# Second layer's first product of a two-layer feed-forward kernel as seven half-size products

## The chip, the cores and the metric

The program runs on one core of a Trainium2 chip. The metric is the device time of one execution in microseconds (us). The core's TensorE (PE) does the matrix products, VectorE (DVE) and ScalarE (ACT) the elementwise work, GpSimd (POOL) a little of the attention, and SyncE (SP) issues all transfers. Products go into PSUM, eight banks of 512 float32 columns on 128 partitions; everything else lies in SBUF.

## The reference

```python
def reference(...):
    x = attention(q, k, v, lam)                  # decayed linear attention
    x = x.transpose(...).reshape(1536, 512)      # tokens x features
    h = x @ moe_w_in                             # layer 1: 512 -> 2048
    x = (h * tanh(softplus(h))) @ moe_w_out      #          2048 -> 512
    h = x @ moe2_w_in                            # layer 2: 512 -> 2048
    g = h * clip(h + 3.0, 0.0, 6.0) / 6.0
    return g @ moe2_w_out                        #          2048 -> 512
```

## The kernel before

The 1536 tokens are three blocks of 512 (k = 0, 1, 2) and the 2048 hidden features sixteen tiles of 128. An operand is kept as two float32r parts, a high one (`split_hi`, ACT) and the rest (`split_lo`, DVE), and a product is three passes over the parts: high-high, high-low, low-high (`PASS`). So one 128x128 weight tile against 512 tokens takes three matmuls.

**Layer 1** is 48 steps of the loop `for n in range(STEPS)`: `gemm1` (12 matmuls of 512 columns, line 328), two steps later `emit_g2` (12 more, line 337), with Mish on ACT between them (lines 357, 358) and `g_lo` on DVE. Blocks 0 and 1 go through tiles 0 to 7 first and leave their sums in `part` ("keep"), block 2 goes through all sixteen and is split at once into X[2] ("split"), then blocks 0 and 1 go through tiles 8 to 15 ("add", line 372), and `split_owed` splits their sums into X[0] and X[1].

From step 21 on `make_later` also prepares layer 2's weights between the steps. Such a unit is one half (0: first product, 1: second product) of one pair p of tiles. `assemble` rebuilds it from its loaded 64-bit form (lines 296 to 302); of the second product's half it makes four sums (line 462). `deliver` splits it into a slot of `low` and spills it to HBM (`wc`). Half 0 has four 128x512 parts of weights, half 1 has seven.

**Layer 2** is 24 runs j, one for each block and pair: block 2, 0, 1, eight pairs each, in turning order so that pairs still in SBUF are used again. Four slots of both halves are held, the others are fetched from `wc` (`swap`). A run's first product (line 609) is two times 12 matmuls of 512 columns into one PSUM bank. `gate` applies relu, min and multiply (lines 632, 633), `sums` makes four sums of the 2x2 blocks of tokens by features (line 643), `parts` splits seven 128x256 blocks (lines 86, 89). The second product (line 625) is already Strassen's scheme (in Winograd's form): seven products m = 1 to 7, each of two times three matmuls of 256 columns, 42 in all, kept in seven PSUM banks through the eight pairs of a block. It follows one run behind the first product: of run j - 1, products 1, 4, 2 stand behind the first half of run j's first product, products 6, 7, 5, 3 behind the second half. At a block's end `close` scales and adds the seven banks into four quarters of the output and stores them.

A scheduler may move instructions on each engine, so the order of the code is only nearly that of the queues.

Of the kernel before, what the change touches and what calls it, by code (L numbers as in the profile page):

```python
# [20 lines left out]
def decay_attention__mish_ffn__hswish_ffn_kernel(  # L21
# [8 lines left out]
    nc = tc.nc  # L30
# [37 lines left out]
    BANKS = {"h": 2, "y": 4, "a": 2}  # L68

    def bank(kind, shape, name):  # L70
        i = bank_turn[kind]
        bank_turn[kind] = (i + 1) % BANKS[kind]
        return ps.tile(shape, F32, tag=f"{kind}{i}", name=name)
# [92 lines left out]
    def scores(c, kind):  # L166
        qT, kT = qk(c)
        sc = [bank(kind, [128, 4, 128], f"sc{h2}") for h2 in range(2)]
# [96 lines left out]
    def load_w(w, t, half, count):  # L265
        if w is w1 and count == 2:
            st = stage_p.tile([128, 2, 512], U64, tag="st2", name="st")
        elif w is w1:
            i = unit_turn[0] % 3
            unit_turn[0] += 1  # L270
            slots[w is w1, t, half] = {i}
            st = ring[:, i:i + 1]
        elif half == 0:
            slots[w is w1, t, half] = {0, 1}
            st = ring[:, 0:2]
        else:
            slots[w is w1, t, half] = {3}
            st = spare[0][:, 8:16].bitcast(U64).rearrange("p a n -> p (a n)").rearrange("p (t n) -> p t n", t=2)
# [33 lines left out]
    def convert(w, t, half, count):  # L312
        hf = to_single(staged(w, t, half))
        cols = slice(half * 512, half * 512 + 512)
        if count == 2:
            whole, i = (low0, t) if t < 2 else (low, t - 2)
            both = whole.rearrange("p (t a n) -> p t a n", a=2, n=1024)[:, i:i + 2, :, cols]
            wh, wl = both[:, :, 0], both[:, :, 1]
        else:
            wh, wl = W[t][:, 0:1, cols], W[t][:, 1:2, cols]  # L320
        split(wh, wl, hf)
# [42 lines left out]

    def evacuate(n, es):
        layer, k, t, first, last, end = seq[n]
        for e in es:
# [5 lines left out]
            else:  # L373
                split_hi(X[k][:, 0, e, :], y)
                split_lo(X[k][:, 1, e, :], X[k][:, 0, e, :], y)
            if end == "add":
                owed.append((k, e))

    owed = []

    def split_owed():
        if owed:
            k, e = owed.pop(0)
            split_hi(X[k][:, 0, e, :], part[k][:, e, :])
            split_lo(X[k][:, 1, e, :], X[k][:, 0, e, :], part[k][:, e, :])

    def emit_g2(n):
        layer, k, t, first, last, end = seq[n]
        if first:
            y_t[:] = [bank("y", [128, 512], "y") for _ in range(4)]  # L390
        gemm2(layer, t, g_t.pop(n), y_t, first, last, range(4))
        if last:
            evacuate(n, range(4))
# [58 lines left out]
    def assemble(u):  # L452
        p, half = later[u]
        B = spare[0] if half else ring[:, 2].bitcast(F32).rearrange("p (a n) -> p a n", n=256)
        whole = B[:, 0:4].rearrange("p (t i) n -> p t (i n)", t=2)
        to_single(staged(w2, 2 * p, half), whole)
        prefetch(u + 3)
        if half == 0:
            ready[u] = whole
        else:  # L460
            for o, x, y in ((4, 0, 1), (5, 2, 4), (6, 2, 0), (7, 3, 5)):
                nc.vector.tensor_tensor(out=B[:, o], in0=B[:, x], in1=B[:, y], op=ALU.subtract)
            ready[u] = B[:, 1:8]

    def deliver(u):
        p, half = later[u]
        c = w2c(p % 2) if half else w1c(p % 2).rearrange("p t a n -> p a t n")
        split(c[:, 0], c[:, 1], ready.pop(u))
        spill(p, half)
# [53 lines left out]
    twice = {24, 27, 31, 35, 39, 43}  # L523
    chunk = {"s": 4, "o": 4}
    for n in range(STEPS):
# [23 lines left out]
        h = bank("h", [128, 512], "h")  # L549
# [21 lines left out]
        split_owed()  # L571
        if n not in conv_first:
            advance(conv_at.get(n, 0))
        if n == 20:
            spare.append(main.tile([128, 16, 256], F32, tag="low0", name="spare"))
            prefetch(2)
        if n >= 21 and PHASES:
            make_later(2 if n in twice else 1)

    SLOT += [(up[0][:, 2048 * i:2048 * i + 2048], up[1 + 2 * i][:, 0:3584]) for i in range(2)]  # L580
    assert not PHASES
    GBUF = [main.tile([128, 4096], F32R, tag="low0", name="G0")[:, 0:3584], up[2][:, 0:3584]]
# [227 lines left out]
```

## Time and profile before

| | us |
|---|---|
| median of 3 timed runs | 584.03 (582.09 to 584.14) |
| profiled execution | 580.44 |
| its span, first to last instruction | 578.7 |
| of this: attention and layer 1 | 0 to 313.6 |
| layer 2, 24 runs | 313.6 to 573.2 |
| last sums and stores | to 578.7 |

The profile is of one execution. Its time is 1.74 us more than its span, and the timed runs lie up to 3.7 us above it. A matmul's end in the records is modelled, so matmuls that follow one another overlap by some 0.16 us in the busy times; the start of one to the start of the next is the safer measure.

### The profile page before, as it was taken

Reading aid. Unit: us, or ns where it says so; the run is one execution under the profiler, and the core shown is the slowest. Engines: PE = TensorE matmul, PEld = TensorE weight load, DVE = VectorE, ACT = ScalarE, POOL = GpSimd, SP = SyncE. Lnnn points to the kernel's source line nnn. Section 1 sums busy time; section 2 is a strip of 40 time slices with the busy share of each in tenths; the row PEclk is TensorE's granted clock in tenths of the full one; section 3 lists DMA queues with packets and bytes.
Section 4 is the critical chain, followed back from the end, with each engine's and each line's share of the span. In section 5 each row is a group of like instructions: output and inputs, shape, how many; then the busy total and the mean of one; then the engine's idle time right before and its main releaser. Section 6 shows DMA issues by size and latency. Waiting matters only on the chain.

```text
span 578.7 us, 8451 instructions
## 1 busy us (share of the span) xinstructions
PE 567.0 (98%) x3470; PEld 479.9 (83%) x3470; DVE 350.2 (61%) x516; ACT 258.5 (45%) x371; POOL 15.6 (3%) x20
## 2 busy tenths in 40 slices
PE   7999999999999999999999999999999999999996
PEld 3777787778888888888888888899989988999895
DVE  3799963465747677675881645355654554754555
ACT  2379733345756557565751333233232333332332
POOL 1600100000000000000000000000000000000000
PEclk9999999999999999999999999999999999999999
DMA  7968622422445879667896568400487300585302
GB/s 236 410 235 294 243 75 74 182 74 91 141 170 218 321 297 323 272 219 297 323 362 256 199 232 312 183 1 1 146 306 294 128 0 19 185 323 221 128 1 73
DMA packets 23168, 113.80 MB, mean 197 GB/s; under 512 B 2122, under 2 KB 6234, under 8 KB 17498
## 3 DMA queue, kind: packets, MB, share of 16 engines
q1 hardware_dynamic: 23130, 113.26, 53.0%
q8 instruction: 27, 0.44, 0.3%
q14 instruction: 11, 0.09, 0.1%
HBM read 87.03 MB, written 26.22 MB: 196 GB/s over the span
## 4 chain that ended last, share of the span: by engine, by line
PE 86%; DVE 5%; ACT 3%; DMA 2%; POOL 1%; issue 1%; DVEq 0%; SPq 0%; POOLq 0%; ACTq 0%
PE h L609 22%; PE h L328 21%; PE y L337 20%; PE acc L625 20%; ACT st L296 1%; PE uo L217 1%; DMA mask<-z 1%; PE sc L172 1%; PE uo L226 1%; PE uo L210 1%; DVE low L89 1%; POOL raw L188 1%; POOL raw L190 0%; DVE X L89 0%; DVE raw L195 0%
## 5 line engine op out<-in xcount | busy, mean ns | idle before, releaser
L633 DVE SCALAR_TENSOR_TENSOR F<-x,h 128x512 f32<-128x512 f32 x48 | 33.0, 687 | 95.1 <-ACT x L632 95.0
L632 ACT ACTIVATE x<-h 128x512 f32<-128x512 f32 x48 | 28.7, 598 | 124.9 <-PE h L609 124.7
L328 PE MATMUL h<-X,low 128*128 128x512 f32 x288 | 71.9, 397 | 0.2 <-DVE state L249 0.2
L609 PE MATMUL h<-X,up 128*128 128x512 f32 x288 | 70.0, 392 | 0.3 <-DVE F L633 0.3
L337 PE MATMUL y<-g,low 128*128 128x512 f32 x288 | 69.8, 390 | 0.1
L609 PE MATMUL h<-X,low 128*128 128x512 f32 x288 | 69.8, 391 | 0.0
L328 PE MATMUL h<-X,up 128*128 128x512 f32 x288 | 69.2, 389 | 0.0
L337 PE MATMUL y<-g,up 128*128 128x512 f32 x288 | 69.2, 389 | 0.0
L337 PEld LDWEIGHTS y<-g,low 128*128 128x128 f32 x288 | 53.9, 188 | 12.1 <-DVE low L89 1.0
L328 PEld LDWEIGHTS h<-X,low 128*128 128x128 f32 x288 | 52.9, 188 | 13.2 <-issue 1.9
L328 PEld LDWEIGHTS h<-X,up 128*128 128x128 f32 x288 | 54.1, 188 | 11.2
L337 PEld LDWEIGHTS y<-g,up 128*128 128x128 f32 x288 | 54.1, 188 | 11.2
L609 PEld LDWEIGHTS h<-X,up 128*128 128x128 f32 x288 | 52.5, 188 | 10.4 <-DVE F L633 0.5
L609 PEld LDWEIGHTS h<-X,low 128*128 128x128 f32 x288 | 52.7, 188 | 10.0
L357 ACT ACTIVATE x<-h 128x512 f32<-128x512 f32 x48 | 28.5, 594 | 65.8 <-PE h L328 65.8
L89 DVE TENSOR_TENSOR g<-x,g 128x512 fp32r<-128x512 f32 x48 | 33.0, 687 | 41.0 <-ACT g L358 40.9
L296 ACT ACTIVATE ring<-ring 128x512 f32<-128x512 f32 (+3 forms) x52 | 40.0, 826 | 14.3 <-DMA ring<-w 14.3
L643 DVE TENSOR_TENSOR F<-F 128x256 f32<-128x256 f32 x96 | 40.6, 423 | 2.2
L86 ACT ACTIVATE up<-F 128x768 fp32r<-128x768 f32 (+3 forms) x27 | 23.5, 871 | 25.4 <-DVE F L643 15.6
L86 ACT ACTIVATE G<-F 128x768 fp32r<-128x768 f32 (+1 forms) x24 | 22.9, 954 | 25.7 <-DVE F L643 16.6
L89 DVE TENSOR_TENSOR up<-F,up 128x768 fp32r<-128x768 f32 (+3 forms) x27 | 26.6, 988 | 12.4 <-ACT up L86 12.4
L625 PEld LDWEIGHTS acc<-low,G 128*128 128x128 f32 x252 | 31.9, 191 | 1.8 <-ACT G L86 0.6
(65 smaller groups left out, 692.1 us busy)
## 6 DMA issues: line engine op xcount, KB each, us to landing
wc<-low SPq DMA_DIRECT2D x8, 1792.0 KB, 6.7
up<-wc SPq DMA_DIRECT2D x8, 1792.0 KB, 7.4
raw<-att SPq DMA_DIRECT2D x24, 512.0 KB, 6.4
low<-wc SPq DMA_DIRECT2D x6, 1792.0 KB, 7.3
ring<-w SPq DMA_DIRECT2D x18, 512.0 KB, 5.0
ring<-w SPq DMA_DIRECT2D x8, 1024.0 KB, 5.0
spare<-w SPq DMA_DIRECT2D x8, 1024.0 KB, 6.1
wc<-low SPq DMA_DIRECT2D x8, 1024.0 KB, 8.8
```

What stands on the lines that cost most here:

```text
L86: nc.scalar.activation(out=hi, in_=src, func=ACTF.Copy)
L89: nc.vector.tensor_tensor(out=lo, in0=src, in1=f32(hi), op=ALU.subtract)
L172: nc.tensor.matmul(sc[h2][:, p, :], lhsT=kT[r, p, :], rhs=qT[r, p, :], start=True, stop=True)
L296: ins = nc.scalar.activation(out=o, in_=i, func=ACTF.Copy, scale=scale, bias=bias)
L328: nc.tensor.matmul(h, lhsT=W[t][:, a, kt * 128:kt * 128 + 128], rhs=X[k][:, b, kt, :], start=(kt, a, b) == order[0], stop=(kt, a, b) == or ...
L337: nc.tensor.matmul(y[e], lhsT=l, rhs=r, start=(first and i == 0), stop=(last and i == 2),)
L357: nc.scalar.activation(out=x, in_=h, func=ACTF.Mish)
L609: nc.tensor.matmul(h, lhsT=w[:, a, kt * 128:kt * 128 + 128], rhs=X[k][:, b, kt, :], start=(kt, a, b) == order[0], stop=(kt, a, b) == order ...
L625: nc.tensor.matmul(acc[m][:, s], lhsT=G[:, a, gi, s * 128:s * 128 + 128], rhs=w[:, b, wi], start=(first and s == 0 and i == 0), stop=(last ...
L632: nc.scalar.activation(out=x, in_=h, func=ACTF.Relu, bias=3.0)
L633: nc.vector.scalar_tensor_tensor(out=F[:, 2 * i:2 * i + 2].rearrange("p i n -> p (i n)"), in0=x, scalar=6.0, in1=h, op0=ALU.min, op1=ALU.mult,
L643: nc.vector.tensor_tensor(out=F[:, o], in0=F[:, a], in1=F[:, b], op=op)
```

## The change

The first product of layer 2 becomes seven products as well: tokens (512 into 2x256), input features (512 into 2x256) and hidden features (2 tiles) are halved. Each is 128 features by 256 tokens over 256 inputs: two tiles times three passes, six matmuls of 256 columns, 42 a run in place of 24 of 512. The operands are seven sums of the weights (`WSUMS`, now for half 0 too, so both halves are alike: seven parts, 1792 KB) and seven of the tokens (`token_sums`, in `XC`). They go in four fills, a (product 1), b (2, 6), c (7, 5) and d (4, 3), through bank 0 one after the other. Each is copied out by ACT, DVE adds the copies up into the two tiles' 2x2 blocks `FH`, and the gate then works in SBUF. Behind each fill stand products of the second product, which now lags by two runs (`LAG`). The units of weights are reordered (the half-0 units of the last two pairs come last), six slots of one unit are held, and four fetches are issued within layer 1 (`EARLY`).

```diff
-    BANKS = {"h": 2, "y": 4, "a": 2}
+    BANKS = {"h": (0, 1), "y": (2, 3, 4, 5), "a": (6, 7)}
...
+    GROUP_BANKS = [(2, 3, 4, 5)] * 3 + [(6, 7, 2, 3), (4, 5, 6, 7)]
...
+        if end == "split":
+            y = BANK[:, b:b + 4]
+            nc.scalar.activation(out=tmp[:, 0], in_=y[:, 0:2, 256:512], func=ACTF.Copy)
+            for _ in token_sums(k, y, tmp):
+                pass
...
+    def token_sums(k, y, tmp=None):     # seven put, four sub, one at a time
+        def sub(o, a, b):
+            nc.vector.tensor_tensor(out=o, in0=a, in1=b, op=ALU.subtract)
+        def put(i, src):
+            split(xs[i][:, 0], xs[i][:, 1], src)
...
+    later = [(p, half) for p in range(NPAIR - 2) for half in (0, 1)]
+    later += [(p, half) for half in (1, 0) for p in (NPAIR - 2, NPAIR - 1)]
...
     def assemble(u):
-        if half == 0:
-            ready[u] = whole
-        else:
-            for o, x, y in ((4, 0, 1), (5, 2, 4), (6, 2, 0), (7, 3, 5)):
+        for o, x, y, op in WSUMS[half]:
+            nc.vector.tensor_tensor(out=B[:, o], in0=B[:, x], in1=B[:, y], op=op)
+        ready[u] = B[:, 1:8]
     def deliver(u):
-        split(c[:, 0], c[:, 1], ready.pop(u))
-        spill(p, half)
+        split(c[:, :, 0], c[:, :, 1], ready.pop(u))
+        spill(later[u], u % 2)
...
+    EARLY = {43: ((3, (NPAIR - 3, 0)),), 45: ((4, (NPAIR - 1, 1)),), 47: ((5, (NPAIR - 2, 1)), (2, (NPAIR - 4, 0)))}
...
-        split_owed()
...
+    LAG = 2
+    FILLS = (("a", (1,)), ("b", (2, 6)), ("c", (7, 5)), ("d", (4, 3)))
+    ACC = {1: 2, 4: 3, 2: 1, 6: 4, 7: 5, 5: 6, 3: 7}
+    def fill(j, ms, bank_):
+        for i, m in enumerate(ms):
+            for kt in range(2):
+                for q, (a, b) in enumerate(PASS):
+                    nc.tensor.matmul(
+                        bank_[:, 256 * i:256 * i + 256], lhsT=w[:, a, kt * 128:kt * 128 + 128], rhs=x[:, b, kt],
...
+    GAPS = ((1,), (4, 2), (6, 7), (5, 3))
+    for j in range(R):
+        if j == 0:
+            prepare.append(token_sums(0, part[0]))
+        if j == NPAIR + 1:
+            prepare.append(token_sums(1, part[1]))
+        for f, (name, ms) in enumerate(FILLS):
+            bank_ = BANK[:, f % 2 if j < LAG else 0]
+            fill(j, ms, bank_)
+            nc.scalar.activation(out=c, in_=bank_[:, 0:n], func=ACTF.Copy)
+            if f == 1:    # one add of 512 columns; f == 2: of 512 and 256; f == 3: of 512
...
+            if j < LAG:
+                emit_g2(STEPS - 2 + j, [f])
+            else:
+                second(j - LAG, GAPS[f])
+            if f == 0 and j > 0:
+                gate(j - 1, 0, 3)
+                feature_sums(j - 1)
+            elif f == 1 and j > 0:
+                feature_parts(j - 1)
+            elif f == 3:
+                gate(j, 1, 1)
+            if f in (1, 3):
+                for g in prepare:
+                    next(g, None)
+        for x in swaps.get(j, ()):
+            fetch(*x)
```

TensorE's queue in run 3 of layer 2 before: two halves of the first product (L609, 12 matmuls each), each followed by products of the second (L625).

```order
L609 MATMUL h_2782<-X2_78,up0_81 128x512 [waits DMAHW4_49,DVE_49]
L609 MATMUL h_2782<-X2_78,up0_81 128x512 x11
L625 MATMUL acc1_2618<-up1_818,G0_2520 128x256 [waits DMAHW0_49,Activation_49]
L625 MATMUL acc1_2618<-up1_818,G0_2520 128x256
L625 MATMUL acc1_2618<-up1_818,G0_2520 128x256 [waits DVE_49]
L625 MATMUL acc1_2618<-up1_818,G0_2520 128x256 x3
L625 MATMUL acc4_2625<-up1_818,G0_2520 128x256 x6
L625 MATMUL acc2_2632<-up1_818,G0_2520 128x256 x6
L609 MATMUL h_2817<-X2_78,up0_81 128x512 [waits DVE_49]
L609 MATMUL h_2817<-X2_78,up0_81 128x512 x11
```

TensorE's queue after the change in run 8 (the first run of block 0), from fill a (L698 is `fill`, L712 `second`).

```order
L698 MATMUL bank_76<-X0_77,lowA_81 128x256 [waits Activation_49]
L698 MATMUL bank_76<-X0_77,lowA_81 128x256 x5
L712 MATMUL bank_76<-up0_82,lowB_2453 128x256 [waits DMAHW6_49]
L712 MATMUL bank_76<-up0_82,lowB_2453 128x256
L712 MATMUL bank_76<-up0_82,lowB_2453 128x256 [waits DVE_49]
L712 MATMUL bank_76<-up0_82,lowB_2453 128x256 x3
L698 MATMUL bank_76<-X0_77,lowA_81 128x256 [waits Activation_49]
L698 MATMUL bank_76<-X0_77,lowA_81 128x256 x5
L698 MATMUL bank_76<-X1_78,lowA_81 128x256 x6
L712 MATMUL bank_76<-up0_82,lowB_2453 128x256 x12
L698 MATMUL bank_76<-X1_78,lowA_81 128x256 [waits Activation_49]
```

Between two fills stand six or twelve matmuls of the second product, and each fill's first matmul waits for ACT, which copies the fill before it out of the same bank.

The same queue in run 7, from fill a.

```order
L698 MATMUL bank_76<-X2_79,lowA_81 128x256 [waits DMAHW4_49,Activation_49]
L698 MATMUL bank_76<-X2_79,lowA_81 128x256 x5
L698 MATMUL bank_76<-X2_79,lowA_81 128x256 [waits Activation_49]
L698 MATMUL bank_76<-X2_79,lowA_81 128x256 x5
L698 MATMUL bank_76<-lowA_81 128x256 x6
L712 MATMUL bank_76<-lowA_81,up3_1228 128x256 [waits DMAHW5_49]
L712 MATMUL bank_76<-lowA_81,up3_1228 128x256
L712 MATMUL bank_76<-lowA_81,up3_1228 128x256 [waits DVE_49]
L712 MATMUL bank_76<-lowA_81,up3_1228 128x256 x15
```

Here the scheduler has put fill b directly behind fill a, and the six matmuls of product 1 behind fill b; so it is, in whole or in part, in runs 4, 5 and 7.

ScalarE's queue after the change through run 6 (L813 copies fills out, L722 is the gate's relu, L88 `split_hi`).

```order
L813 ACTIVATE work_2457<-bank_76 128x256 [waits PE_49,Activation_49]
L88 ACTIVATE lowB_2453<-work_2457 128x3x256 [waits DVE_49]
L813 ACTIVATE work_2457<-bank_76 128x512 [waits PE_49,Activation_49]
L88 ACTIVATE lowB_2453<-FS1_2540 128x4x256 [waits DVE_49]
L813 ACTIVATE two_2458<-bank_76 128x512 [waits PE_49,Activation_49]
L722 ACTIVATE x_3056<-work_2457 128x512 [waits DVE_49,Activation_49]
L813 ACTIVATE two_2458<-bank_76 128x512 [waits PE_49,Activation_49]
L722 ACTIVATE x_3074<-work_2457 128x512 [waits DVE_49]
L813 ACTIVATE work_2457<-bank_76 128x256 [waits PE_49,Activation_49]
```

The four copies a, b, c, d of a run stand in one queue with two splits and two relus, each of which waits for DVE; before, this queue held two relus and two splits a run and no copy.

## Rows read from the trace of the kernel before

**Rows 1.** The page: busy us of each engine (share of the span, instructions)
```profile
PE 567.0 (98%) x3470; PEld 479.9 (83%) x3470; DVE 350.2 (61%) x516; ACT 258.5 (45%) x371; POOL 15.6 (3%) x20
```
**Rows 2.** Stages by windows: length, busy us of each engine, clock, DMA share, GB/s
```profile
224.00:313.60 89.60, 89.60 (x397) 74.20 (x396) 62.26 (x78) 51.66 (x68) 0.00 (x0) 1.00 0.81 303
313.60:347.00 33.40, 32.69 (x182) 28.27 (x181) 17.42 (x30) 10.31 (x15) 0.00 (x0) 1.00 0.51 188
347.00:557.50 210.50, 210.50 (x1323) 190.92 (x1322) 111.06 (x175) 65.44 (x86) 0.00 (x0) 1.00 0.42 155
```
**Rows 3.** The chain that ended last, one run of layer 2 and its end: start, us
```profile
354.80 2.87 PE acc L625 x24
357.67 2.75 PE h L609 x12
360.42 2.15 PE acc L625 x18
...
565.30 5.05 PE acc L625 x42
```
**Rows 4.** Timeline of TensorE where layer 2 begins: start, us, what
```profile
313.61 2.88 PE L609 MATMUL h<-X,low 128*128 128x512 f32 x12
...
324.49 2.88 PE L609 MATMUL h<-X,low 128*128 128x512 f32 x12
...
336.34 0.96 PE L609 MATMUL h<-X,up 128*128 128x512 f32 x3 [0.28 <-DVE F L633]
```
**Rows 5.** The chain where TensorE waits in run 1: start, us, what
```profile
329.86 0.04 issue
329.90 1.22 PE acc L625 x8
```
**Rows 6.** Timeline near the end, a first product's half and its gate
```profile
560.24 2.32 PE L625 MATMUL acc<-up,G 128*128 128x256 f32 x18
560.50 0.60 ACT L632 ACTIVATE x<-h 128x512 f32<-128x512 f32 x1 [1.00 <-PE h L609]
561.13 0.69 DVE L633 SCALAR_TENSOR_TENSOR F<-x,h 128x512 f32<-128x512 f32 x1 [0.37 <-ACT x L632]
```
**Rows 7.** Groups by shape, whole span: count, busy us and mean ns, idle before
```profile
L632 ACT ACTIVATE x<-h 128x512 f32<-128x512 f32 x48 | 28.7, 598 | 124.9 <-PE h L609 124.7
L643 DVE TENSOR_TENSOR F<-F 128x256 f32<-128x256 f32 x96 | 40.6, 423 | 2.2
L89 DVE TENSOR_TENSOR G<-F,G 128x1024 fp32r<-128x1024 f32 x12 | 14.7, 1225 | 10.1 <-ACT G L86 10.1
L86 ACT ACTIVATE G<-F 128x1024 fp32r<-128x1024 f32 x12 | 12.7, 1060 | 16.6 <-DVE F L643 16.6
L89 DVE TENSOR_TENSOR G<-F,G 128x768 fp32r<-128x768 f32 x12 | 11.5, 960 | 0.0
L86 ACT ACTIVATE G<-F 128x768 fp32r<-128x768 f32 x12 | 10.2, 848 | 9.1 <-DVE F L633 9.1
L86 ACT ACTIVATE X<-uo 128x256 fp32r<-128x256 f32 x24 | 8.6, 380 | 23.8 <-PE uo L226 16.4 <-DVE state L251 5.7 <-PE uo L217 1.0
L89 DVE TENSOR_TENSOR X<-part,X 128x512 fp32r<-128x512 f32 x8 | 5.4, 684 | 0.0
```
**Rows 8.** Groups of the preparation of layer 2's weights, whole span
```profile
L462 DVE TENSOR_TENSOR spare<-spare 128x256 f32<-128x256 f32 x32 | 12.1, 419 | 0.2
L89 DVE TENSOR_TENSOR low<-spare,low 128x1792 fp32r<-128x1792 f32 x8 | 16.2, 2024 | 8.6 <-ACT low L86 8.6
L89 DVE TENSOR_TENSOR low<-ring,low 128x1024 fp32r<-128x1024 f32 x8 | 9.7, 1219 | 0.5 <-ACT low L86 0.5
```
**Rows 9.** Timeline of DVE: the last unit of weights delivered
```profile
300.91 2.03 DVE L89 TENSOR_TENSOR low<-spare,low 128x1792 fp32r<-128x1792 f32 x1 [1.77 <-ACT low L86]
```
**Rows 10.** DMA issues: queue, count, KB each, median us from issue to landing
```profile
wc<-low SPq DMA_DIRECT2D x8, 1792.0 KB, 6.7
up<-wc SPq DMA_DIRECT2D x8, 1792.0 KB, 7.4
```

More of the change, by code (lines that the diff above doesn't have):

```diff
@@ L167, in scores @@
         qT, kT = qk(c)
-        sc = [bank(kind, [128, 4, 128], f"sc{h2}") for h2 in range(2)]
+        sc = [bank(kind, [128, 4, 128]) for h2 in range(2)]
         for p in range(4):
@@ L201, in attend @@
         kn, vn = kv(c)
-        uo = [bank(kind, [128, 2, 256], f"uo{i}") for i in range(2)]
+        uo = [bank(kind, [128, 2, 256]) for i in range(2)]
         u = uo[0][:, 1].rearrange("p (a d) -> p a d", a=4)
@@ L391, in emit_g2 @@
-        gemm2(layer, t, g_t.pop(n), y_t, first, last, range(4))
+        if first and es[0] == 0:
+            y_t[:] = [BANK[:, i] for i in GROUP_BANKS[group_turn[0]]]
+            group_turn[0] += 1
+        gemm2(layer, t, g_t[n], y_t, first, last, es)
         if last:
-            evacuate(n, range(4))
+            evacuate(n, es)
     def order(w, tiles, lead=2):
@@ L614, in second_product, with upcoming @@
-    def second_product(j, which):
+    R = len(runs)
+    LAG = 2
+    need = [set() for _ in range(R + LAG)]
+    for j, (k, p) in enumerate(runs):
+        need[j].add((p, 0))
+        need[j + LAG].add((p, 1))
+    def upcoming(j):
+        seen = []
+        for t in range(j, R + LAG):
+            seen += [x for x in sorted(need[t], key=lambda x: x[1]) if x not in seen]
+        return seen
+    where = {(NPAIR - 2, 0): 0, (NPAIR - 1, 0): 1, **{x: slot for e in EARLY.values() for slot, x in e}}
@@ new lines, in second, with gate, feature_sums @@
+                        start=(first and i == 0 and q == 0), stop=(last and q == 2), skip_group_check=True,
+                    )
+            if last:
+                close(k, m)
+    def gate(j, lo, step):
+        F = FH[j % 2][:, lo:lo + step + 1:step]
+        x = tm2_p.tile([128, 2, 256], F32, tag="x", name="x")
+        nc.scalar.activation(out=x, in_=F, func=ACTF.Relu, bias=3.0)
+        nc.vector.scalar_tensor_tensor(out=F, in0=x, scalar=6.0, in1=F, op0=ALU.min, op1=ALU.mult)
+    def feature_sums(j):
+        F, S = FH[j % 2], FS[j % 2]
+        A21, A11, A22, A12 = (F[:, i] for i in range(4))
+        for o, a, b, op in (
+            (0, A21, A22, ALU.add), (2, A11, A21, ALU.subtract), (1, S[:, 0], A11, ALU.subtract),
+            (3, A12, S[:, 1], ALU.subtract),
+        ):
+            nc.vector.tensor_tensor(out=S[:, o], in0=a, in1=b, op=op)
@@ L764 @@
+    gate(R - 1, 0, 3)
+    second(R - 2, (1, 4, 2))
+    feature_sums(R - 1)
+    feature_parts(R - 1)
+    second(R - 2, (6, 7, 5, 3))
+    for x in swaps.get(R, ()):
+        fetch(*x)
+    second(R - 1, (1, 7, 6, 5, 4, 2, 3))
 def kernel(**inputs):
```

365 lines of the change are left out of this document (183 added, 182 removed).

## Prediction

> **What bounds the kernel now.** The page comes first: TensorE is busy 98% of the span, DVE 61%, ACT 45% [rows 1]. Then the stages: from 347 to 557.5 us TensorE is busy all of 210.50 us at granted clock 1.00 (the 2.4 GHz level), DVE 111.06 us of it and ACT 65.44 us [rows 2]. So in layer 2's steady part nothing but the number and pitch of matmuls counts, and only as long as no other engine makes TensorE wait. The pitch is read from the chain, since it goes from start to start: 12 matmuls of 512 columns take 2.75 us (229 ns each), 18 and 24 of 256 columns take 2.15 and 2.87 us (119.5 ns each), and 42 in a row at the end 5.05 us (120 ns) [rows 3]. A run is 2.75 + 2.15 + 2.75 + 2.87 = 10.52 us. A second loss stands where layer 2 starts: run 1 goes from 324.49 to 336.34 us, 11.85 us, 1.3 us more than a run [rows 4], since the second product waits there for the splits of the run just before it [rows 5].
>
> **1. Fewer columns.** Each run's first product goes from 24 x 229 ns = 5.50 us to 42 x 120 ns = 5.05 us, so -0.45 us a run and -10.8 us in 24 runs. By the smaller pitch of 119.5 ns it is -11.5 us. The other end: in layer 1 a stretch of 24 matmuls of 512 columns has a pitch of 5.44 us (313.61 to 324.49 is two such, 10.88 [rows 4]); if a run's 24 cost that, its 42 of 256 columns cost 10.52 - 5.44 = 5.08, and the saving is 0.36 a run, -8.6 us. I take -10.8, as the row of 42 in a row is nearest to a queue that holds 256-column matmuls alone.
>
> The Trainium skill (TensorE: Matmul & The Clock Gate, Back-to-back issue gap) gives the gap of warm matmuls as columns / 2.4 + 2.5 ns. By it, an estimate from that page, 24 gaps of 215.8 ns against 42 of 109.2 ns would save 0.59 us a run, 14.2 us in all. The rows show 10 to 13 ns more on each matmul of either size, and halved matmuls pay that nearly twice as often, so the rows' 10.8 stands.
>
> **2. The lag of two runs.** The wait of 1.3 us in run 1 goes, because the splits of run 0 are now wanted two runs later: -1.3 us. Runs 0 and 1 hold fills and the last layer-1 products (5.05 + 12 x 0.227 = 7.8 us each) while DVE has some 7.7 us of work a run there (step 3), four adds of 0.68 and what is left of the token sums; put one after the other, the first run's splits end about 0.8 us before they are wanted. If they don't, up to 1.3 us comes back.
>
> **3. Copies through one bank.** This is the wait that the change adds: a fill may begin only when ACT has copied out the fill before it, and ACT's queue holds, behind each copy, a relu or a split that waits for DVE. From a product's last matmul to ACT's start takes 0.26 us (the next matmul starts at 560.24, the relu at 560.50), ACT to DVE 0.03 [rows 6], ACT to TensorE 0.04 [rows 5]. A copy of 512 columns out of PSUM is near the relu's 0.598, one of 256 near the 0.380 of the X split [rows 7]. So a fill's bank is free 0.26 + 0.60 + 0.04 = 0.90 us after b or c, and 0.26 + 0.38 + 0.04 = 0.68 us after a. The cover: twelve matmuls of the second product, 1.44 us, behind b, c, d, but six, 0.72 us, behind a. The chain before copy a must be in time too. Count from the end of fill d: copy d 0.26 to 0.86, DVE's last add to 1.58, relu to 2.21; fill a ends at 1.44 + 0.72 = 2.16, so its copy starts at 2.42, after the relu, and ends at 2.80, and fill b is due at 2.88. Fits, by 0.04. Further on: gate on DVE to 2.9; split of three blocks on ACT (0.85) to 3.8; copy b 4.58 to 5.18, due 5.72; four sums and the first split's rest to 5.7; split of four blocks (1.06) to 6.8; copy c 7.46 to 8.06, due 8.6. Fits. I set 0.3 us for all runs; if copy a costs 0.598 instead, it is 0.18 us a run (rival A).
>
> DVE's work a run goes from 5.25 us (two gates, four sums of 0.423, splits of 0.960 and 1.225 [rows 7]) to 7.73 us with three adds of 0.69 and one of 0.42: 77% of 10.1 us. ACT goes from 3.1 to 5.3 us (three copies of 0.60, one of 0.38). Both lie beside TensorE.
>
> In runs 4, 5 and 7 the queue has fill b directly behind fill a, without the six matmuls between. There TensorE waits the whole 0.68 to 0.71 us: +2.1 us. The six come later, but no wait is there for them to fill.
>
> **4. Token sums.** For block 1 they stand in runs 7 and 8: seven splits and four subtractions of 512 columns, on DVE 11 x 0.684 = 7.5 us [rows 7] on top of 2 x 7.73, more than two runs of 10.1 us. Followed along the queues, DVE's add after copy d comes 1.4 us late, relu and copy a behind it, and fill b starts 0.4 and 0.5 us late in runs 8 and 9: +0.9 us (0 to 3). The end of a block (seven DVE operations of 0.69 in run 9, and in run 17) adds 0.2. For blocks 2 and 0 they fall into layer 1 (step 5).
>
> **5. Preparation.** The four sums of half 0 (4 x 0.419 = 1.68 us) and its longer split (2.024 - 1.219 = 0.81) [rows 8] are 2.5 us more DVE work for each of eight pairs. From 224 us on, DVE is busy 62.26 of 89.60 us [rows 2]; some five pairs are done there, +12.4, and token sums of blocks 2 and 0 add about 9.6: 84 of 89.6 us. The last unit was delivered at 302.9 us [rows 9], and was wanted late; now the last one is the first that layer 2 reads, at 313.6. Walked through the queue, it ends near 311: cover 3 us. One `g_lo`, behind the token sums of block 2, is wanted only 0.4 us after its end. I set +0.5 for both and the start (0 to 5). The early fetch of a slot stands in SP's queue ahead of a spill and waits for TensorE; the spill is read two runs later.
>
> **6. Transfers.** A run in mid-block needs two new units of 1792 KB, and each is freed two runs, 20 us, before it is read. One lands in 7.4 us [rows 10], two one after the other in 14.8. Zero, and up to 2 us if they slow each other.
>
> **7. The end.** The last run's splits follow fill d by copy, add, relu, gate, four sums and two splits, 7.9 us, against 54 + 6 matmuls, 7.2 us, to the first one that needs the second split's low part: +0.5. The last closing sums are as before.
>
> **The sum** against the profiled execution, 580.44 us: -10.8 - 1.3 + 0.3 + 2.1 + 0.9 + 0.2 + 0.5 + 0.5 = -7.6, so 572.8. The median of the timed runs is 3.6 us above that execution, which I carry over: 584.03 - 7.6 = **576.4 us**, 1.3% less.
>
> **The rivals.** (A) One bank binds at fill b. The Trainium skill's advice (Perfetto Trace Analysis, Matmuls) is that independent groups should rotate through PSUM banks so that evacuation overlaps the next group's matmuls; here the cover is the other product. If copy a costs 0.6 and some hops more, 0.2 us a run in 22 runs: +4.4, 580.8. For it: a margin of 0.04. Against it: the 0.380 of a 256-column read from PSUM [rows 7]. (B) The preparation comes late: DVE at 94% and transfers at share 0.81 [rows 2] leave little; 5 us of waiting at 313.6 and at Mish: 581.4. (C) Slower than before: ACT falls behind in every run, because a split that waits for DVE stands ahead of a copy. Then each run loses about the 0.85 us split [rows 7] less some cover, 0.6 us: 24 x 0.6 = 14.4, 590.8. It is slower from 7.6 / 24 = 0.32 us a run on. For it: the copies stand behind DVE-bound instructions in one queue. Against it: the timetable of step 3, with 0.5 us to spare at b, c and d. (D) Alone in the queue, 256-column matmuls come down to half of the 229 ns: 42 x 0.1145 = 4.81 us, 0.69 a run, 16.6 in all, 5.8 more than in the sum: 570.6. Against it: 120 ns in the row of 42 [rows 3]. The Trainium skill's gap (the page and section of step 1) points to this side.
>
> **How the numbers follow.** The forecast has 0.62, A 0.15, B 0.08, C 0.10, D 0.05. A measurement tells some 0.5% here, so faster means below 581.1 and slower above 587. Forecast: 0.58 faster, 0.04 same. D is faster. A lies at the border: 0.07 and 0.08. B: 0.02 faster, 0.05 same, 0.01 slower. C is slower. Together 0.72, 0.17, 0.11. The range goes from 571.5 (saving 11.5, hardly a stall) to 583 (saving 8.6 with stalls of 6 to 7 us, A, B).
>
> **What would show it.** Steady runs of 10.1 us start to start; busy TensorE with no idle ahead of the second fill but in runs 4, 5, 7 to 9; the wait of run 1 gone; the fills' copies at 0.38 and 0.60. Wrong would be: idle TensorE ahead of fills in every run, released by ACT (A, C), or a gap near 313 us (B).

## The result and the profile after

The changed kernel takes 575.32 us (median of 4 runs, 575.03 to 576.56) against 583.40 us before (582.09 to 584.14): a ratio of 0.9868, 95% interval 0.9843 to 0.9893. Run again beside the kernel before it took 575.60 against 581.87 us, 0.9879 (0.9858 to 0.9900). The forecast was 576.4 us. The profiled execution took 575.03 us, its span is 573.3 us.

The page's first line, and its busy times, engine by engine (compare [rows 1]):

```profile
span 573.3 us, 9666 instructions
PE 558.8 (97%) x3902; PEld 494.8 (86%) x3902; DVE 430.4 (75%) x664; ACT 320.4 (56%) x476; POOL 15.7 (3%) x20
```

VectorE went from 61% to 75%, ScalarE from 45% to 56%, and TensorE is still the bound. The stages in windows (length; busy us of PE, PEld, DVE, ACT, POOL; clock; DMA share; GB/s), the first two as in [rows 2], the third cut at 552:

```profile
224.00:313.60 89.60, 89.60 (x397) 74.20 (x396) 82.00 (x113) 61.12 (x78) 0.00 (x0) 1.00 0.83 322
313.60:347.00 33.40, 33.40 (x252) 32.08 (x251) 24.95 (x43) 16.95 (x28) 0.00 (x0) 1.00 0.95 385
347.00:552.00 205.00, 203.20 (x1675) 201.71 (x1674) 159.63 (x266) 111.98 (x173) 0.00 (x0) 1.00 0.76 289
```

TensorE is idle for 1.8 of the 205 us where it was idle for nothing before. What it waited for in layer 2 (engine, line, releaser: us in all, times, longest):

```profile
PE bank L698 <- ACT work L813: 1.6, 3, 0.5
PE bank L712 <- DVE up L91: 0.2, 1, 0.2
```

L698 is a fill's matmul, L813 the copy out of the bank. The timeline of TensorE (start, us; a row's last matmul is drawn longer than its share of the pitch, so read from start to start) gives the first fill of run 0, 1 and 2, where [rows 4] had runs of 10.88 and 11.85 us:

```profile
315.19 0.88 PE L698 MATMUL bank<-X,lowA 128*128 128x256 f32 x6
...
322.99 0.87 PE L698 MATMUL bank<-X,lowA 128*128 128x256 f32 x6
...
330.77 0.87 PE L698 MATMUL bank<-X,up 128*128 128x256 f32 x6
```

Runs 0 and 1 are 7.80 and 7.78 us, with no wait. Runs 2 and 3 take 10.08 us each, 84 matmuls of 0.120 us and nothing else. Most later ones take 10.15 or 10.16 (11 and 19 take 10.09). Run 12, with the weight loads and ScalarE's copies beside it, shows the difference:

```profile
435.07 0.88 PE L698 MATMUL bank<-X,lowA 128*128 128x256 f32 x6
435.68 0.79 PEld L712 LDWEIGHTS bank<-up,lowB 128*128 128x128 f32 x6
435.79 0.88 PE L712 MATMUL bank<-up,lowB 128*128 128x256 f32 x6
436.05 0.39 ACT L813 ACTIVATE work<-bank 128x256 f32<-128x256 f32 x1 [0.17 <-PE bank L698]
436.49 1.49 PEld L698 LDWEIGHTS bank<-X,lowA 128*128 128x128 f32 x12
436.51 1.68 PE L698 MATMUL bank<-X,lowA 128*128 128x256 f32 x12
437.91 0.79 PEld L712 LDWEIGHTS bank<-up,lowB 128*128 128x128 f32 x6
438.03 1.60 PE L712 MATMUL bank<-up,lowB 128*128 128x256 f32 x12
```

Copy a ends at 436.44, and fill b's matmul at 436.51 looks on time. But its weight load, which stands 0.11 or 0.12 us ahead of the matmul in the other rows (435.68 and 435.79, 437.91 and 438.03), comes only at 436.49, 0.05 us behind the copy. So twelve matmuls take 1.52 us from start to start instead of 1.44. Nothing is idle by the page, but 0.08 us is lost.

In run 4 fill b stands in part directly behind fill a, and the copy is waited for in full (1.42 us from start to start, 0.70 more than the 0.72 of six matmuls; runs 5 and 7 have the same row at 363.21 and 384.22):

```profile
350.93 0.88 PE L698 MATMUL bank<-X,lowA 128*128 128x256 f32 x6
352.35 0.62 PE L698 MATMUL bank<-X,lowA 128*128 128x256 f32 x3 [0.53 <-ACT work L813]
```

Runs 4, 5 and 7 take 10.86 us; runs 8 and 9, where the token sums of block 1 stand, 10.65 and 10.51. The end, where the last fill's splits are late for the second of the two closing products:

```profile
556.85 5.20 PE L712 MATMUL bank<-up,lowB 128*128 128x256 f32 x42
561.89 1.12 PE L712 MATMUL bank<-lowA,up 128*128 128x256 f32 x8
563.19 4.34 PE L712 MATMUL bank<-lowA,up 128*128 128x256 f32 x34 [0.17 <-DVE up L91]
```

Layer 2 now starts at 315.19 us, 1.58 us later than in [rows 4]. So the span's 5.4 us are 7.0 us gained in layer 2 (265.1 to 258.1 us from its first fill to the end of the span) and 1.6 us lost ahead of it.

### The profile page after: what moved, and what is told of

Its sections match the earlier page's. It is cut to its first block, busy times and chain, and to the rows that moved or that the text cites. A ratio compares the mean times of both kernels' runs of the same rounds, so it can differ in the third digit from the quotient of the medians.

```text
span 573.3 us, 9666 instructions
## 1 busy us (share of the span) xinstructions
PE 558.8 (97%) x3902; PEld 494.8 (86%) x3902; DVE 430.4 (75%) x664; ACT 320.4 (56%) x476; POOL 15.7 (3%) x20
## 4 chain that ended last, share of the span: by engine, by line
PE 84%; DVE 5%; ACT 4%; DMA 4%; issue 1%; POOL 1%; DVEq 0%; SPq 0%; ACTq 0%; POOLq 0%
PE bank L337 21%; PE bank L328 21%; PE bank L698 20%; PE bank L712 18%; DMA st<-w 2%; ACT st L296 2%; PE bank L219 1%; PE bank L174 1%; DMA mask<-z 1%; PE bank L212 1%; PE bank L228 1%; DVE rest L751 1%; DVE FS L732 0%; POOL raw L190 0%; DVE X L91 0%
## 5 line engine op out<-in xcount | busy, mean ns | idle before, releaser
L337 PE MATMUL bank<-g,up 128*128 128x512 f32 x288 | 70.3, 389 | 0.0
L328 PE MATMUL bank<-X,up 128*128 128x512 f32 x288 | 69.2, 389 | 0.0
L328 PEld LDWEIGHTS bank<-X,up 128*128 128x128 f32 x288 | 54.1, 188 | 11.2
L337 PEld LDWEIGHTS bank<-g,up 128*128 128x128 f32 x288 | 53.6, 188 | 10.6
L698 PE MATMUL bank<-X,up 128*128 128x256 f32 x384 | 55.5, 286 | 0.6 <-ACT work L813 0.5
L722 ACT ACTIVATE x<-work 128x512 f32<-128x512 f32 x48 | 30.3, 632 | 40.5 <-DVE work L823 24.5
L698 PEld LDWEIGHTS bank<-X,up 128*128 128x128 f32 x384 | 49.6, 191 | 1.5 <-ACT work L813 1.0
L813 ACT ACTIVATE two<-bank 128x512 f32<-128x512 f32 x48 | 28.6, 596 | 34.1 <-PE bank L698 34.1
L296 ACT ACTIVATE ring<-ring 128x512 f32<-128x512 f32 (+3 forms) x52 | 39.7, 820 | 10.7 <-DMA ring<-w 10.6
L328 PE MATMUL bank<-X,lowA 128*128 128x512 f32 x180 | 45.2, 397 | 0.0
L337 PE MATMUL bank<-g,lowA 128*128 128x512 f32 x180 | 43.3, 389 | 0.0
L712 PE MATMUL bank<-up,lowB 128*128 128x256 f32 x318 | 42.9, 283 | 0.0
L712 PEld LDWEIGHTS bank<-up,lowB 128*128 128x128 f32 x318 | 40.2, 192 | 0.0
L328 PEld LDWEIGHTS bank<-X,lowA 128*128 128x128 f32 x180 | 33.1, 188 | 8.2 <-issue 1.2
L698 PE MATMUL bank<-X,lowA 128*128 128x256 f32 x270 | 38.9, 285 | 1.2 <-ACT work L813 1.1
L813 ACT ACTIVATE work<-bank 128x256 f32<-128x256 f32 (+1 forms) x48 | 23.5, 490 | 27.8 <-PE bank L698 27.4
L712 PE MATMUL bank<-up,up 128*128 128x256 f32 x276 | 37.7, 283 | 0.0
L698 PEld LDWEIGHTS bank<-X,lowA 128*128 128x128 f32 x270 | 35.1, 191 | 2.2 <-ACT work L813 1.8
```

What stands on the lines that cost most here:

```text
L296: ins = nc.scalar.activation(out=o, in_=i, func=ACTF.Copy, scale=scale, bias=bias)
L328: nc.tensor.matmul(h, lhsT=W[t][:, a, kt * 128:kt * 128 + 128], rhs=X[k][:, b, kt, :], start=(kt, a, b) == order[0], stop=(kt, a, b) == or ...
L337: nc.tensor.matmul(y[e], lhsT=l, rhs=r, start=(first and i == 0), stop=(last and i == 2),)
L698: nc.tensor.matmul(bank_[:, 256 * i:256 * i + 256], lhsT=w[:, a, kt * 128:kt * 128 + 128], rhs=x[:, b, kt], start=(i == 0 and kt == 0 and ...
L712: nc.tensor.matmul(acc[:, i], lhsT=GB[j % 2][:, gi, a, i * 128:i * 128 + 128], rhs=w[:, b], start=(first and i == 0 and q == 0), stop=(las ...
L722: nc.scalar.activation(out=x, in_=F, func=ACTF.Relu, bias=3.0)
```

## The experiments

The table holds each kernel's first layer-1 product, the first fill of layer 2, the end of the span, the length of layer 2 (the third minus the second) and the median of its runs. Layer 2's length repeats to 0.1 us where a kernel was traced twice, and is what the comparisons below go by.

| kernel | first product | layer 2 from | span | layer 2 | median us |
|---|---|---|---|---|---|
| before | 29.08 | 313.61 | 578.7 | 265.1 | 583.40 |
| e8_before_again | 30.57 | 315.23 | 580.4 | 265.2 | 582.17 (one run) |
| changed | 30.31 | 315.19 | 573.3 | 258.1 | 575.32 |
| e7_after_again | 30.20 | 316.25 | 574.3 | 258.1 | 575.60 |
| e1_order | 29.16 | 315.78 | 575.7 | 259.9 | 576.89 |
| e2_gaps | 29.84 | 314.78 | 575.1 | 260.3 | 577.21 |
| e3_wide_copy | 30.24 | 314.91 | 578.6 | 263.7 | 580.33 |
| e4_halves | 28.81 | 313.85 | 585.4 | 271.6 | 588.08 |
| e5_queues | 29.40 | 316.23 | 573.7 | 257.5 | 575.44 |
| e6_all_three | 28.44 | 314.88 | 570.2 | 255.3 | 571.99 |
| e9_two_splits | 29.16 | 313.99 | 579.1 | 265.1 | 580.90 (one run) |
| e10_late_pins | 28.36 | 314.75 | 568.9 | 254.2 | 571.08 |

**e1_order: TensorE's order held.**

```diff
+                    ins = nc.tensor.matmul(bank_[:, 256 * i:256 * i + 256], ...)
+                    tc.keep_in_program_order(ins)
...
+                    ins = nc.tensor.matmul(acc[:, i], ...)
+                    tc.keep_in_program_order(ins)
```

> The changed kernel, but with TensorE's instructions of layer 2 held in the order fill a, product 1, fill b in every run. Theory: in runs 4, 5 and 7 fill b stands (in part) directly behind fill a and waits 0.70 us for the copy of a; with product 1 between, these three runs go from 10.86 us to the 10.15 us of the others, 2.1 us in all, from 575.3 to 573.2 us. Rival: product 1 could not have started there (its weights or splits come late), so the wait only changes place; TensorE then stands ahead of product 1, released by a transfer or by VectorE, and the time stays at 575.3 us.

Measured: 576.89 us (575.92 to 577.53), layer 2 1.8 us longer than in the changed kernel. Ahead of fill b the wait is gone (0.08 us is left, as in the other runs), but run 4 takes 11.35 us. TensorE in run 4 (product 1 and fill c) and ScalarE beside it:

```profile
354.48 1.60 PE L713 MATMUL bank<-lowA,lowB 128*128 128x256 f32 x12
357.03 0.98 PE L698 MATMUL bank<-lowA 128*128 128x256 f32 x6 [0.95 <-ACT work L815]
```

```profile
353.10 0.85 ACT L88 ACTIVATE up<-work 128x768 fp32r<-128x768 f32 x1 [0.21 <-DVE work L725]
355.44 1.06 ACT L88 ACTIVATE up<-FS 128x1024 fp32r<-128x1024 f32 x1 [1.49 <-DVE FS L734]
356.40 0.58 ACT L815 ACTIVATE work<-bank 128x512 f32<-128x512 f32 x1
```

ScalarE in the changed kernel, in the same run:

```profile
352.50 0.85 ACT L88 ACTIVATE up<-work 128x768 fp32r<-128x768 f32 x1 [0.21 <-DVE work L723]
354.85 0.60 ACT L813 ACTIVATE work<-bank 128x512 f32<-128x512 f32 x1 [1.50 <-PE bank L698]
355.35 1.05 ACT L88 ACTIVATE up<-FS 128x1024 fp32r<-128x1024 f32 x1
```

Copy b and the split of four blocks have changed places. Once TensorE's order was another, the scheduler put the split first; it waits for VectorE's sums until 355.44, the copy stands behind it until 356.40, and fill c waits 0.95 us (1.20 in run 7) instead of fill b 0.53. The expectation named two ways out, and it was neither: product 1 could start, and the gain came at fill b, but a new wait took more than it gave.

**e2_gaps: the cover shared out evenly.**

```diff
-    GAPS = ((1,), (4, 2), (6, 7), (5, 3))
+    GAPS = ((1, 4.0), (4.1, 2, 6.0), (6.1, 7, 5.0), (5.1, 3))
...
+            halves = range(2)
+            if isinstance(m, float):
+                halves = (round(10 * m) % 10,)
+                m = int(m)
```

> As e1_order, and the 42 matmuls of the second product are shared out between the four fills as 9, 12, 12, 9 instead of 6, 12, 12, 12, product 4, 6 and 5 being cut in their two halves. Theory: the 0.07 to 0.08 us that each run takes above 42 + 42 matmuls of 0.120 us is fill b's first weight load waiting for copy a; with nine matmuls (1.08 us) of cover it goes, runs take 10.08 us, and some 20 runs give 1.4 to 1.6 us: from 573.2 (if e1 comes out so) to 571.7 us. Copy d keeps 1.08 us of cover against a chain of 0.26 + 0.60 + 0.05 + 0.12 = 1.03 us, just enough. Rival: the 0.07 is a price of TensorE's own, for turning from one product to the other; then the runs stay at 10.15 us and the time at 573.2 us.

Measured: 577.21 us (576.16 to 578.81). The steady run does what the theory says, from 436.69 to 446.77, 10.08 us, and fill b's twelve matmuls go by without a loss:

```profile
436.69 0.88 PE L698 MATMUL bank<-X,lowA 128*128 128x256 f32 x6
437.41 1.24 PE L717 MATMUL bank<-up,lowB 128*128 128x256 f32 x9
438.49 1.60 PE L698 MATMUL bank<-X,lowA 128*128 128x256 f32 x12
...
446.77 0.88 PE L698 MATMUL bank<-X,up 128*128 128x256 f32 x6
```

So the 0.08 us is the copy's chain and not TensorE's own price. The total does not show it: runs 4 and 5 keep e1's wait ahead of fill c, in run 7 it is 1.54 us, and run 17, with the closing sums of a block, takes 10.70 us.

**e3_wide_copy: the copy behind fill a made longer.**

```diff
-            nc.scalar.activation(out=c, in_=bank_[:, 0:n], func=ACTF.Copy)
+            if f == 0 and j >= LAG:
+                nc.scalar.activation(out=work[:, 2048:2560], in_=bank_, func=ACTF.Copy)
+            else:
+                nc.scalar.activation(out=c, in_=bank_[:, 0:n], func=ACTF.Copy)
```

> As e1_order, but ScalarE copies all 512 columns of the bank behind fill a where 256 are needed (the other 256 columns are thrown away), so that this copy takes 0.60 instead of 0.39 us. Theory: the bank's chain behind fill a has no margin left, so the 0.21 us come back in full in each of the 22 runs that have a second product: runs of 10.36 us, 4.6 us in all, 573.2 + 4.6 = 577.8 us. Rival: the 0.07 us of a run is TensorE's own and copy a still has the 0.04 us of margin that the sum gave it; then the runs lose 0.17 in all, 10.25 us, and the time is 575.4 us.

Measured: 580.33 us (578.72 to 581.40), 3.8 us more in layer 2 than e1. Steady runs take 10.36 or 10.37 us, 0.21 more, to the hundredth what the longer copy costs. Its rows:

```profile
438.60 0.88 PE L713 MATMUL bank<-up,lowB 128*128 128x256 f32 x6
438.86 0.60 ACT L816 ACTIVATE work<-bank 128x512 f32<-128x512 f32 x1 [0.23 <-PE bank L698]
439.51 1.70 PE L698 MATMUL bank<-X,lowA 128*128 128x256 f32 x12
```

There was no margin of 0.04 us to eat first. The total is 0.8 us short of 4.6, since in the runs with another wait the two overlap in part.

**e4_halves: the kernel before, with the first product's matmuls cut in two.**

```diff
-        for kt, a, b in order:
-            nc.tensor.matmul(h, lhsT=..., rhs=X[k][:, b, kt, :], ...)
+        for n in (slice(0, 256), slice(256, 512)):
+            for kt, a, b in order:
+                nc.tensor.matmul(h[:, n], lhsT=..., rhs=X[k][:, b, kt, n], ...)
```

> The kernel before, with each matmul of the second layer's first product cut in two of 256 columns (48 instead of 24 a run, the same columns in all, no Strassen scheme in it). Theory: a matmul of 256 columns has a pitch of 0.120 us wherever it stands, against 0.229 for 512, so 48 take 5.76 us against 5.50: 0.26 us a run, 6.3 us in 24 runs, 583.4 + 6.3 = 589.7 us. Rival: the pitch of 0.120 belongs to the second product's operands and a matmul of the first product halves to 0.1145 us; then the time stays at 583.4 us.

Measured: 588.08 us (587.17 to 589.43), a ratio of 1.0107 (1.0079 to 1.0136), and layer 2 longer by 6.4 us, where 6.3 were expected. In its chain (start, us, what) 24 halves take 2.88 us where [rows 3] has 2.75 for 12 whole ones:

```profile
402.11 2.88 PE h L610 x24
404.99 2.16 PE acc L626 x18
407.15 2.88 PE h L610 x24
```

The pitch of 0.120 us belongs to a matmul of 256 columns of this kind, not to the second product. The Trainium skill (TensorE: Matmul & The Clock Gate, Back-to-back issue gap) has 109.2 and 215.8 ns for the two sizes, by its formula for an isolated matmul; an estimate from that page is 1.5 us for this edit. The trace disagrees: it shows 6.4 us.

**e5_queues: the other two queues held as well.** A helper chains each instruction of layer 2 to the one written before it on its engine:

```diff
+    def pin(at):
+        for i in nc.cur_bb.bb.instructions[at:]:
...
+            if e in pinned_last:
+                tc.add_manual_dep(i, pinned_last[e], mybir.DependencyInfo(
+                    mybir.DependencyClass.NoSync, mybir.DependencyReason.DATA))
+            pinned_last[e] = i.name
```

> As e1_order, and in layer 2 the instructions of ScalarE and VectorE (copies, adds, gates, sums, splits; not the token sums and not the closing sums) stand in the order of the program too, so that the copy of fill b stands ahead of the splits in every run. Theory: what e1 gained ahead of fill b in runs 4, 5 and 7 it lost again ahead of fill c (0.95, 0.95 and 1.20 us of idle TensorE), because ScalarE had the split of four blocks, which waits for VectorE's sums, ahead of copy b there; with the copy first these waits go too, and layer 2 is 2.1 us shorter than in the changed kernel: 573.2 us against 575.3. Rival: copies are late in these runs for another reason (VectorE behind, or the transfers); then idle time of about 1 us stays ahead of a fill in runs 4, 5 and 7 and the time stays near 576 us.

Measured: 575.44 us (575.25 to 576.25), layer 2 shorter by 0.6 us instead of 2.1. Runs 4, 5 and 7 take 10.15, 10.16 and 10.29 us: the 2.1 us came (2.0), and the wait at fill c is gone, which settles e1's loss. But run 2 takes 11.09 us (10.08 before), and run 8 11.10 (10.65). Run 2, TensorE and ScalarE:

```profile
332.52 0.88 PE L714 MATMUL bank<-up,lowB 128*128 128x256 f32 x6
334.17 0.98 PE L700 MATMUL bank<-X,up 128*128 128x256 f32 x6 [0.77 <-ACT work L837]
```

```profile
333.21 0.63 ACT L724 ACTIVATE x<-work 128x512 f32<-128x512 f32 x1 [1.24 <-DVE work L847]
333.75 0.37 ACT L837 ACTIVATE work<-bank 128x256 f32<-128x256 f32 x1
```

Fill a was done at 332.52, but in the written order the gate's relu of the run before stands ahead of copy a. It waits for VectorE until 333.21, because VectorE has that run's adds to the layer-1 sums in its queue too. In the changed kernel the scheduler had put copy a first (at 331.68). In run 8 copy a begins only at 395.45, behind the same kind of relu (394.40, after 1.18 us of waiting for VectorE) and behind a split of token sums (394.94).

**e6_all_three: e5, the even cover, and the token sums at a later place.**

```diff
-        if j == NPAIR + 1:
+        if j == NPAIR + 2:
             prepare.append(token_sums(1, part[1]))
...
+                if j > NPAIR and SPREAD:
+                    pin(at)
```

> As e5_queues, with the 9, 12, 12, 9 matmuls of e2_gaps behind the fills, and the token sums of block 1 held in VectorE's queue where the program writes them, two steps a run from run 10 on, instead of being drawn into runs 7 and 8. Theory: on top of the 2.1 us of e5, 22 runs lose 0.07 to 0.08 us less (1.6 us), and the waits of runs 8 and 9 go (0.50 + 0.36 = 0.86 us): 575.3 - 4.6 = 570.7 us, every run from 2 on at 10.08 us. Rival: VectorE's 7.73 us a run plus 1.37 of token sums comes late somewhere (block ends in runs 9 and 17 add seven operations), so runs 9 to 16 show idle TensorE ahead of a fill, 0.3 us or more each, and the time is 573 us or above.

Measured: 571.99 us (571.59 to 573.27), a ratio of 0.9833 (0.9813 to 0.9852) to the kernel before, and layer 2 2.8 us shorter than in the changed kernel. Runs 3 to 9 take 10.08 us, 8 and 9 among them, so the waits of these two were the token sums': the even cover alone (e2) and the held queues alone (e5) left run 8 at 10.70 and 11.10. What is left are 0.41 us of idle TensorE in run 2 (as in e5) and 0.40 in run 10, where token sums follow close on a block's closing sums: the rival, in one run of the eight it named.

**e10_late_pins: the same, without what was left.**

```diff
     def pin(at):
+        if now[0] < 3:
+            return
...
-        if j == NPAIR + 2:
+        if j == NPAIR + 3:
...
-            if f in (1, 3):
+            if f in (1, 3) or f == 2 and j > NPAIR:
```

> As e6_all_three, but the order of the program holds from run 3 on only (run 2 is left to the scheduler), and the token sums of block 1 begin in run 11, behind the closing sums of the block before, three steps a run. Theory: the two waits left in e6, 0.57 us in run 2 (copy a behind a gate's relu that the pinned order put ahead) and 0.56 us in run 10 (closing sums and token sums together), go: layer 2 takes 254.2 us from its first fill to the end instead of 255.3, and the time is 570.9 us. Rival: three steps of token sums a run are too many for VectorE, and runs 11 to 14 wait 0.3 us or more each: layer 2 at 255.3 us or above, 572 us.

Measured: 571.08 us (568.66 to 574.68), a ratio of 0.9817 (0.9784 to 0.9851) to the kernel before, layer 2 254.2 us as expected. Runs 2 to 22 take 10.07 or 10.08 us but for runs 10 (10.20) and 18 (10.21). The same window as above has TensorE busy all through:

```profile
347.00:552.00 205.00, 205.00 (x1709) 204.83 (x1708) 163.11 (x268) 106.00 (x175) 0.00 (x0) 1.00 0.76 288
```

This is the shortest layer 2 of all; the medians of e6 and e10 lie closer together than the runs of e10 scatter. VectorE is busy for longer in the window than in the changed kernel (163.11 against 159.63 us) and costs nothing there; only its order is another. With runs of 10.08 us one PSUM bank for the fills is enough, so the advice to rotate banks (the Trainium skill, Perfetto Trace Analysis, Matmuls) was not needed here: nine to twelve matmuls of other work cover an evacuation.

**e7, e8 and e9: the first layer.** Two kernels traced again as they are, and the kernel before with one edit:

> The changed kernel as it is, once more, beside e5 and e6 on the same chip, and for a second trace of its first 315 us. Theory: the 1.6 us by which layer 2 started later than in the kernel before lie for 1.2 us ahead of the first product (30.31 against 29.08 us), where both kernels run the same instructions and wait for the transfer of the mask, so they are scatter from run to run: the start of the first product lands anywhere in 28.8 to 30.3 us again, time 575.3 us. Rival: the change makes the start later; then it stands near 30.3 us again and above all that the kernel before shows.

> The kernel before as it is, for a second trace of its first layer. Theory (scatter): the first product starts anywhere in 28.8 to 30.3 us and layer 2 at 313.6 to 315 us. Rival (the change delays the start): 28.8 to 29.1 us and 313.6 to 313.9 us, as in the two traces with this first layer.

> The kernel before, where only the weights' third and fourth tiles are split one after the other (two splits of 512 columns on ScalarE and VectorE each) instead of by one of 1024, as the changed kernel has to do since these tiles lie in two buffers there. Theory: in every trace of the changed first layer TensorE waits 0.4 to 1.0 us near 64 us ahead of the scores, released by VectorE's split of X, and in neither trace of the kernel before; the two splits in place of one make VectorE's queue there later, so the wait appears here too, and layer 2 starts 284.7 + 0.4 to 1.0 us after the first product. Rival: the wait comes from elsewhere in the change (another order of the queues, transfers); then there is none here, and layer 2 starts 284.7 us after the first product, as in the two traces of the kernel before (284.5 and 284.7).

```diff
+        if count == 2 and t == 2:
+            for i in range(2):
+                split(W[t + i][:, 0:1, cols], W[t + i][:, 1:2, cols], hf[:, i:i + 1])
+        else:
             split(wh, wl, hf)
```

The first product of the kernel before, traced again:

```profile
30.57 1.62 PE L328 MATMUL h<-X,low 128*128 128x512 f32 x6 [0.20 <-DVE state L249]
```

The start of the first product is scatter, as the theory had it: 28.8 to 30.6 us with the first layer of before (four traces, counting e9 with its one edit), 28.4 to 30.3 with the changed one (eight). e7's 30.20 alone would have fitted its rival; the 30.57 of e8 and the 28.4 of e6 and e10 do not, so the rivals of e7 and e8 fall.

But from the first product to layer 2 the traces before, e8, e4 and e9 take 284.5, 284.7, 285.0 and 284.8 us, and the eight of the changed first layer 284.7 to 286.8, 285.9 on average: 1.1 us more. This is not a loss in every trace: the changed kernel's first trace, e2 and e3 take 284.7 to 284.9, and the other five lose 1.3 to 2.1.

All eight show TensorE waiting 0.4 to 2.1 us ahead of the scores near 64 us, released by VectorE's split of X, as in e10, the longest:

```profile
64.30 1.49 PE L176 MATMUL bank<-raw 64*128 64x128 f32 x16 [2.14 <-DVE X L93]
```

The traces of before, e8 and e4 do not show this wait. e9 does: 0.59 us, within its theory's range.

```profile
62.99 0.76 DVE L89 TENSOR_TENSOR X<-uo,X 128x256 fp32r<-128x256 f32 x2
63.52 1.44 PE L172 MATMUL sc<-raw 64*128 64x128 f32 x16 [0.59 <-issue]
```

The profile names no releaser here, but the scores begin 0.53 us after the split of X, as in the changed kernel's first trace (64.01 and 64.50, 0.49 us). Yet e9 takes 284.8 us from the first product to layer 2, which is the rival's figure. So cutting the split in two is not the cause by itself: with it a wait of this size appears at this place, and the first layer stays within the 0.5 us over which the four traces spread. The three changed traces that lose nothing, with waits of 0.4 to 0.7 us there, say the same of the wait.

What the five that lose have in common is a late transfer of weights. ScalarE's longest wait for a transfer into `st` between 28 and 60 us is 0.6 to 1.2 us in the seven traces without a loss and 2.0 to 3.4 us in these five. In the changed kernel's first trace and in e5:

```profile
44.95 2.24 ACT L296 ACTIVATE st<-st 128x1024 f32<-128x1024 f32 x2 [1.18 <-DMA st<-w]
```

```profile
45.97 2.16 ACT L298 ACTIVATE st<-st 128x1024 f32<-128x1024 f32 x2 [3.12 <-DMA st<-w]
```

Both were issued 9.3 us after the first product (39.65 and 38.73). Why the transfer lands late there is not shown, nor that the change makes it so: five of eight traces against none of four can still be scatter. The cause of that 1.1 us stays open.

## Why the forecast held, step by step

The time is 1.1 us from the forecast and the sign is right; the steps are mostly right in kind, and a miss of the base hid, by luck, that the sum was too good.

1. **Fewer columns**, -10.8: right. A run without a wait takes 10.08 us instead of 10.52, so 24 x 0.44 = 10.6 us. The pitch is 0.120 us, as [rows 3] had it in the row of 42 in a row, and e4 confirms it from the other side. Rival D (0.1145 us) is out.
2. **The lag of two runs**, -1.3: right. Run 1 takes 7.78 us, without a wait.
3. **Copies through one bank**, +0.3 and +2.1: the mechanism right, the first size off. The working counted the chain behind fill a as 0.26 + 0.38 + 0.04 = 0.68 us against 0.72, to the start of the next matmul. But what waits for the bank is the weight load ahead of that matmul. With 0.05 to the weight load and the 0.11 us that it leads by, the chain is 0.26 + 0.39 + 0.05 + 0.11 = 0.81, and the fill is 0.07 to 0.08 us late, in runs 6, 8 to 10, 12 to 18 and 20 to 23, fifteen in all: 1.1 us instead of 0.3. That is rival A in kind at less than half its price; e3 shows A's own case (a copy of 0.60) at 0.21 us more. Runs 4, 5 and 7 lose 0.78 us each, 0.70 for the wait and the same 0.08: 2.3 instead of 2.1. That the reordered six matmuls "come later, but no wait is there for them to fill" held, but the plain repair did not (e1): the split that waits for VectorE ahead of a copy, rival C's mechanism, was one change of order away.
4. **Token sums**, +0.9: right. Runs 8 and 9 lose 0.50 and 0.36 us against 10.15, and e6, which moves the sums, has both at 10.08. The +0.2 for the block ends is not seen: run 17 takes 10.15 us like its neighbours, and what the block end adds in run 9 can't be told from the token sums.
5. **Preparation**, +0.5: too much in layer 2, where nothing waits, and in the wrong place. VectorE is busy 82.00 us between 224 and 313.6 (84 foreseen). The last unit's split is done at 312.02 us (311 foreseen), against the first fill at 315.19:

```profile
309.99 2.03 DVE L91 TENSOR_TENSOR lowA<-spare,lowA 128x1792 fp32r<-128x1792 f32 x1 [0.90 <-ACT lowA L88]
```

   The first layer as such was taken as unchanged apart from VectorE's added work. It lost 0.35 us in the two traces compared here (284.53 against 284.88 us from the first product to layer 2) and 1.1 us on average, by a cause that is open (e9).
6. **Transfers**, 0: right. A fetch into `up` takes 9.8 us to land instead of 7.4 [rows 10], at a DMA share of 0.76 instead of 0.42 [rows 2], and no matmul of layer 2 waits for one.
7. **The end**, +0.5: 0.34 us at 563.19, and 0.4 more from the last matmul to the end of the span (573.3 - 567.3 = 6.0 against 578.7 - 573.1 = 5.6): +0.7.

**The sum.** By these, layer 2 changes by -10.6 - 1.3 + 1.1 + 2.3 + 0.9 + 0.7 = -6.9 us, the two traces have 265.1 - 258.1 = 7.0 less, and the forecast had -7.6 (the 0.5 of step 5 counted to layer 2). **What failed is the base**: the 3.6 us between the profiled execution and the median were carried over. They were scatter from run to run: in the changed kernel the profiled execution and the median are 0.3 us apart, and the kernel before took 582.17 us in e8 with the same 265.2 us in layer 2. Of this scatter the traces show 1.5 us in the start of the first product (29.08 and 30.57); no execution near 584 us was traced. Against the profiled execution the forecast was 572.8 and 575.03 was measured, too low by 2.2 us: 1.6 ahead of layer 2 (1.2 of it in the start of the first product) and 0.6 in it. The 3.6 us on top turned that into 1.1 us too high. So the step from the trace to the median was wrong, and hid that the sum was too good. How close the forecast came depends on the base as well: against the first runs of the kernel before the gain is 8.1 us (583.40 to 575.32), against the eleven beside e7 it is 6.3 (581.87 to 575.60), and 7.6 were forecast. Rivals B and C did not come.

## What to carry to other kernels

A buffer's turnaround on TensorE is to be counted up to the weight load, not up to the matmul, and a lateness of less than that lead shows only in starts that are further apart, not as idle time (in e3 even 0.29 us a run are not drawn as idle). Where the cover of several evacuations comes from one pool of work, share it out by what each needs. An order that is mended on one engine has to be looked at on the others as well, and a stage's own length, from its first instruction to the end, tells 0.1 us where the whole time scatters by several.

## What the runs showed of the hardware

ScalarE begins copy a 0.26 us after the fill's last matmul has made way for the next (435.79 to 436.05) in most runs of the changed kernel, and 0.20 us after it in runs 2, 3, 11 and 19. In run 3 product 1 follows fill a at 341.57, and ScalarE has just ended a relu:

```profile
341.08 0.63 ACT L722 ACTIVATE x<-work 128x512 f32<-128x512 f32 x1 [0.87 <-DVE work L825]
341.77 0.38 ACT L813 ACTIVATE work<-bank 128x256 f32<-128x256 f32 x1
```

In run 2 product 1 follows at 331.48, and the copy begins 0.20 us later too, though ScalarE had been idle for 0.75 us:

```profile
331.68 0.38 ACT L813 ACTIVATE work<-bank 128x256 f32<-128x256 f32 x1 [0.75 <-PE bank L698]
```

So whether ScalarE was busy just before does not decide it, and what does stays open. These four runs are the ones that lose nearly nothing at fill b (10.08 or 10.09 us); the 0.06 us is most of what the others lose there.
